# A fused linear-attention and ELU-MLP kernel: paced loads, fewer load buffers, and four output blocks of the first tile at once

## The chip, the core and the metric

The kernel runs on one core of a Trainium2 chip. TensorE (PE) multiplies, VectorE (DVE) and ScalarE (ACT) work on tiles elementwise, GpSimd (POOL) does a few elementwise products and issues the casting loads, SyncE (SP) issues the output stores and the transposes that the DMA crossbar makes. The metric is the device time of one execution in microseconds (us); lower is better.

## The reference

Two layers. The first is linear attention with decay, in 4 batches of 8 heads, 768 positions, head size 64. The second is an MLP with an ELU between its two products, 3072 tokens by 512, inner size 2048.

```python
for b in range(nb):                                  # blocks of 64 positions
    intra = einsum('bhic,bhjc->bhij', qb, kb) * Dmask
    intra = einsum('bhij,bhjd->bhid', intra, vb)
    inter = einsum('bhid,bhde->bhie', qb * lam_pow, kv_state)
    out[:, :, sl] = intra + inter
    kb_dec = kb * rev_pow
    kv_state = lam_block * kv_state + einsum('bhsd,bhse->bhde', kb_dec, vb)
x = out.transpose(0, 2, 1, 3).reshape(3072, 512)
h = x @ w_in
g = where(h > 0, h, exp(min(h, 0)) - 1)
return g @ w_out
```

## The kernel before

**Chunks and tiles.** The positions are cut into 24 chunks of 128 positions of one batch: chunk `g` is position block `g // 4` of batch `g % 4`. Seven tiles of 4, 2, 4, 4, 4, 4 and 2 chunks (`TS`) go through the MLP: tile 0 holds chunks 0 to 3, tile 1 chunks 4 and 5, tile 2 chunks 6 to 9, and so on.

**Attention of a chunk.** q, k and v come in natural layout by casting loads from POOL (`emit_load`, L72); `qn`, `kn`, `vn` are 12 buffers of two chunks each, so every chunk has its own. `att_T` transposes q and k on PE (L218) and `att_Te` copies the result to SBUF on ScalarE (L230); for the chunk pairs listed in `XT` (L615) `att_xT` lets the DMA crossbar transpose instead, from SP (L274). `att_S` (L305) makes scores `psS`, `att_mask` (L317) multiplies them by the decay mask into `P` on VectorE, `att_O` (L331, L339) adds `P`·v and q·state into `psO`, `att_X` (L358, L360) copies that to `xt`, the MLP's input. `att_kd` (L292) scales k, `att_U` (L377) makes the state's increment `psU`, `att_st` (L411, L413) adds it, `att_tmp` (L394) makes the decayed old state on POOL for the next chunk of that batch.

**MLP.** `mm1(t, n)` makes block n of 16 of h for tile t in PSUM (`psH`, L430; for tiles of two chunks two blocks in one bank, L445). ScalarE makes `e = exp` (L456) and `r = relu` (L460), VectorE joins them to `g = min(e - 1, r)` (L473); in three blocks of tile 0 VectorE does it from `e` and `psH` in two steps (L468, L471). `mm2(t, i, n)` adds g's block n times w_out's block n into `psM` of output block i (L505); at n = 15 the result is copied (L519, L521) and stored by SP (L522). e, r and the output copies have three buffers each.

**PSUM.** Three tags share the eight banks: S (four banks, two tiles of two), M and H (two banks each). psH of tile 0 alternates between M and H for n below 8; all other psH are in H, psM in M, and in stage B psM of a block above 1 would be in H.

**Order.** Nothing is scheduled by a planner: every engine runs its instructions in the order of this program. First comes a hand-written part for chunks 0 to 3, with `warm` matmuls on constant data between. Then `steps` (L644) lists, in order, a step name, the mm1 of that step and the mm2 of that step; `at` hangs attention work and loads on step names. Steps ('A', 0..15) are tile 0's mm1, ('B', ...) have no mm1, (1, n) to (6, n) belong to tiles 1 to 6, ('E', 0) is the end. Within a step: mm1 with e and r, then what hangs on the step, then g, then the mm2. `visit(g, s0, s1, s2)` hangs a pair's transposes and kd on s0, scores and masks on s1, products, state and copies on s2.

**Loads.** `LOADS` (L113) is the order of all loads on POOL, weights (`wi` in seven pieces, `wo` in four of four blocks) and two kd products among them. The first 17 are issued at once, ten more after the hand-written part, the last eight at steps of tiles 1 and 2 (L641). A load is only held back when POOL's queue for transfers is full.

The lines that a reader needs most:

```python
    NB = 12
    for s, a, b in [((1, 0), 27, 28), ((1, 4), 28, 29), ..., ((2, 9), 34, 35)]:
        at(s, run_loads, LOADS[a:b])
    for s, m1, m2 in steps:
        ...
            er = mm1(t, n, alt=t == 0 and n in (2, 4, 6))
        do(s)
        if er:
            elu(t, n, *er)
        for t2, i2, n2 in m2:
            mm2(t2, i2, n2, "H" if t2 == 0 and m1 is None and i2 > 1 else "M")
```

Of the kernel before, what the change touches and what calls it, by code (L numbers as in the profile page):

```python
# [7 lines left out]
FP32 = mybir.dt.float32  # L8
# [7 lines left out]
def kernel(  # L16
# [39 lines left out]
    NB = 12  # L56
# [56 lines left out]
    LOADS = [(0, 1, 'q'), (0, 1, 'k'), (0, 1, 'v'), (1, 1, 'q'), (1, 1, 'k'), (1, 1, 'v'), (2, 1, 'q'), (2, 1, 'k'), (3, 1, 'q'), (3, 1, 'k'), (2, 1, 'v'), (3, 1, 'v'), ('wi', 0), ('wi', 1), ('wi', 2), ('wi', 3), ('wi', 4), ('wi', 5), ('kd', 0), ('wi', 6), ('kd', 2), ('wo', 0), (4, 2), ('wo', 1), ('wo', 2), ('wo', 3), (6, 2), (8, 2), (10, 2), (12, 2), (14, 2), (16, 2), (18, 2), (20, 2), (22, 2)]  # L113
# [13 lines left out]
    run_loads(LOADS[:17])  # L127
# [54 lines left out]

    def late_up():
        nc.scalar.activation(ks[:], loglam[:], AF.Exp, scale=pos[:, 1:2])
        for hh in range(2):
            r = slice(hh * 64, (hh + 1) * 64)
            nc.scalar.copy(loglam_p[r, :], loglam[r, hh::2])
        nc.scalar.activation(up_p[:], loglam_p[:], AF.Exp, scale=float(L))
# [158 lines left out]
    def att_X(g, n, parts=1):  # L347
# [5 lines left out]
        for j in range(parts):  # L353
            c = slice(j * w, (j + 1) * w)
            dst = xt[t][:, c, i * L : (i + n) * L].rearrange("p h (n l) -> p n h l", n=n)
            if g < B:
                copy = nc.vector.tensor_copy if g == 0 else nc.scalar.copy
                copy(out=dst, in_=po[:, :, c])  # L358
                continue
# [41 lines left out]
    def att_st(g):  # L401
# [5 lines left out]
        for hh in range(2):  # L407
            r = slice(hh * 64, (hh + 1) * 64)
            if c == 0:
                copy = nc.scalar.copy if g in (2,) else nc.vector.tensor_copy  # L410
# [24 lines left out]
    def mm1(t, n, alt=False):  # L435

        MT = TS[t] * L
        if MT == 256:
            if n == 0:
                gt[t] = msb.tile([128, NF, MT], FP16, tag="g", bufs=2, name=f"g{t}")  # L440
            pH = ps.tile([128, 2 * MT], FP32, tag="H", bufs=2, name=f"psH{t}_{n}")
# [35 lines left out]
    def mm2_last(t, i):  # L477
# [4 lines left out]
        for x, (w, tag) in enumerate([(384, 'M'), (128, 'H')]):  # L482
# [7 lines left out]
            o = msb.tile([128, w], FP32, tag="osb", bufs=3, name=f"osl{x}")  # L490
# [6 lines left out]
    def mm2(t, i, n, tag="M"):  # L497
# [15 lines left out]
        o = msb.tile([128, DM], FP32, tag="osb", bufs=3, name=f"osb{t}_{i}")  # L513
# [3 lines left out]
        else:  # L517
# [4 lines left out]
            nc.sync.dma_start(out=out[t0 : t0 + L, :], in_=o[:])  # L522
        psM.pop((t, i))

    def warm(k, tag="M"):
# [4 lines left out]
        for _ in range(k):  # L530
            nc.tensor.matmul(
                pw[:], lhsT=ident16[:], rhs=any16, start=True, stop=True
            )

    warms = []
    any16 = ident16[:].unsqueeze(1).broadcast_to([128, 4, 128])
# [16 lines left out]
    W = [5, 2, 3, 0, 1, 1, 0, 0, 1, 1, 0]  # L553
# [7 lines left out]
    late_up()  # L561
    warm(W[2])
    att_S(0)
    att_mask(0, 2)
    warm(W[3])
    op_T(1, "q")
    op_Te(1, "q")
    warm(W[4])
    op_T(1, "k")
    op_Te(1, "k")  # L570
    att_O(0, 1, "M")
    att_X(0, 1)
    warm(W[5])
    att_S(1)
    att_mask(1, 2)
    op_T(2, "q")
    op_Te(2, "q")
    warm(W[6])
    op_T(2, "k")
    op_Te(2, "k")  # L580
    warm(W[7])
# [3 lines left out]
    att_mask(2, 2)  # L585
    att_O(1, 1, "M")
    att_X(1, 1)
    warm(W[8])
    att_T2(3, "k", "H")
    warm(W[9])  # L590
    att_S(3)
    att_mask(3, 2)
    att_O(2, 1, "M")
    att_X(2, 1)
    late_qs(0, 2)
    warm(W[10])
    for n in range(0):
        mm1_mm(0, n, 0, 3 * L, "MH"[n % 2])
    att_OX2(3, "H")
    for n in range(0, 1):  # L600
        mm1_mm(0, n, 0, 3 * L, "MH"[n % 2])
    late_qs(2, HP)
    for n in range(1):
        mm1_mm(0, n, 3 * L, 4 * L)

    run_loads(LOADS[17:27])
# [8 lines left out]
    XT = {10: (1, 12), 12: (2, 4), 14: (2, 12), 16: (3, 4), 18: (3, 12), 20: (4, 4), 22: (4, 12)}  # L615
# [23 lines left out]
    for g, vs in [(4, (('A', 12), ('A', 14), ('B', 1))), (6, ((1, 0), (1, 4), (1, 6))), (8, ((1, 8), (1, 12), (1, 14))), (10, ((2, 0), (2, 2), (2, 5))), (12, ((2, 8), (2, 10), (2, 13))), (14, ((3, 0), (3, 2), (3, 5))), (16, ((3, 8), (3, 10), (3, 13))), (18, ((4, 0), (4, 2), (4, 5))), (20, ((4, 8), (4, 10), (4, 13))), (22, ((5, 0), (5, 2), (5, 5)))]:  # L639
        visit(g, *vs)  # L640
    for s, a, b in [((1, 0), 27, 28), ((1, 4), 28, 29), ((1, 8), 29, 30), ((1, 12), 30, 31), ((2, 0), 31, 32), ((2, 3), 32, 33), ((2, 6), 33, 34), ((2, 9), 34, 35)]:  # L641
        at(s, run_loads, LOADS[a:b])

# [42 lines left out]
```

## Time and profile before

| what | value |
| --- | --- |
| median of 4 runs | 216.37 us (215.71 to 216.66) |
| the profiled execution | 216.66 us, of which the span from the first to the last instruction is 214.8 us |
| PE busy | 203.2 us, 95% of the span, 1650 matmuls |
| weight loads (PEld) | 105.8 us, 49% |
| VectorE busy | 151.3 us, 70% |
| ScalarE busy | 128.2 us, 60% |
| GpSimd busy | 77.6 us, 36% |
| software-made DMA queue (POOL's loads) | 80208 packets, 13.63 MB written, 85.1% of 16 engines' span |
| hardware-made DMA queue (SP and ScalarE) | 18384 packets, 9.90 MB, 21.3% |

How to read it: busy is the time in which an engine had an instruction running. A matmul is written down with its modelled end, 0.38 us for 512 columns, while the next can start 0.216 us after it, so a full PE row can still hide a slower pace. The chain of waits goes back from the last instruction, at each step to what released it. Step names like (1, 10) are those of `steps`.

### The profile page before, as it was taken

Reading aid. Unit: us, or ns where it says so; the run is one execution under the profiler, and the core shown is the slowest. Engines: PE = TensorE matmul, PEld = TensorE weight load, DVE = VectorE, ACT = ScalarE, POOL = GpSimd, SP = SyncE. Lnnn points to the kernel's source line nnn. Section 1 sums busy time; section 2 is a strip of 40 time slices with the busy share of each in tenths; the row PEclk is TensorE's granted clock in tenths of the full one; section 3 lists DMA queues with packets and bytes.
Section 4 is the critical chain, followed back from the end, with each engine's and each line's share of the span. In section 5 each row is a group of like instructions: output and inputs, shape, how many; then the busy total and the mean of one; then the engine's idle time right before and its main releaser. Section 6 shows DMA issues by size and latency. Waiting matters only on the chain.

```text
span 214.8 us, 4091 instructions
## 1 busy us (share of the span) xinstructions
PE 203.2 (95%) x1650; PEld 105.8 (49%) x1650; DVE 151.3 (70%) x193; ACT 128.2 (60%) x241; POOL 77.6 (36%) x76
## 2 busy tenths in 40 slices
PE   5878979999999999999999999999999999999994
PEld 1343435556764544545444545445445444555543
DVE  6766999976999999997986786765565533423221
ACT  6948798337566767666465566466456567454510
POOL 8999958469398956344400000000000000000000
PEclk9999999999999999999999999999999999999999
DMA  5999999999999999999993313314211011111112
GB/s 38 144 156 184 203 168 196 189 162 143 156 131 155 208 153 167 133 156 179 184 141 82 68 49 92 57 49 102 50 49 52 0 49 49 53 49 49 49 52 99
DMA packets 98756, 23.87 MB, mean 111 GB/s; under 512 B 90928, under 2 KB 95792, under 8 KB 98736
## 3 DMA queue, kind: packets, MB, share of 16 engines
q0 software_dynamic: 80208, 13.63, 85.1%
q1 hardware_dynamic: 18384, 9.90, 21.3%
q8 instruction: 13, 0.21, 0.4%
q10 hardware_dynamic: 144, 0.07, 0.1%
q14 instruction: 7, 0.06, 0.1%
HBM read 27.27 MB, written 6.29 MB: 156 GB/s over the span
## 4 chain that ended last, share of the span: by engine, by line
PE 58%; POOL 16%; DMA 14%; issue 5%; DVE 4%; ACT 0%; POOLq 0%; DVEq 0%
PE psM L505 29%; PE psH L430 15%; PE psH L445 7%; DMA qn<-in_q_dram 5%; DMA kT<-kn 5%; DMA wo<-in_moe_w_out_dram 4%; POOL qn L72 3%; POOL kn L72 3%; POOL vn L72 3%; POOL wi L97 2%; POOL tmp L394 2%; DVE g L473 2%; PE psO L331 2%; POOL kd L292 2%; PE psM L485 2%
## 5 line engine op out<-in xcount | busy, mean ns | idle before, releaser
L473 DVE SCALAR_TENSOR_TENSOR g<-e,r 128x512 f16<-128x512 f32 x93 | 69.1, 760 | 40.4 <-ACT r L460 40.1
L456 ACT ACTIVATE e<-psH 128x512 f32<-128x512 f32 x96 | 57.5, 599 | 63.2 <-PE psH L430 46.5
L505 PE MATMUL psM<-wo,g 128*128 128x512 f16 x368 | 93.8, 380 | 0.9 <-DMA wo<-in_moe_w_out_dram 0.8
L430 PE MATMUL psH<-xt,wi 128*128 128x512 f16 (+2 forms) x324 | 81.2, 376 | 1.0 <-DVE g L471 0.5
L460 ACT ACTIVATE r<-psH 128x512 f16<-128x512 f32 x93 | 55.3, 595 | 0.1
L505 PEld LDWEIGHTS <-g 128*128 128x128 f16 x368 | 34.3, 98 | 38.5 <-DMA wo<-in_moe_w_out_dram 1.3
L430 PEld LDWEIGHTS <-wi 128*128 128x128 f16 x324 | 31.2, 98 | 38.8 <-issue 1.2
L317 DVE TENSOR_TENSOR P<-psS,mask 128x1024 f16<-128x1024 f32 (+1 forms) x28 | 28.7, 1065 | 4.1 <-PE psS L305 3.9
L394 POOL TENSOR_TENSOR tmp<-st,up_p 64x512 f32<-64x512 f16 x16 | 20.1, 1259 | 14.2 <-DVE st L413 13.4
L72 POOL DMA_DIRECT2D vn<-in_v_dram x14 | 15.2, 1095 | 5.5 <-issue 4.4
L72 POOL DMA_DIRECT2D qn<-in_q_dram x14 | 15.6, 1116 | 4.1 <-issue 3.7
L72 POOL DMA_DIRECT2D kn<-in_k_dram x14 | 15.3, 1092 | 4.5 <-issue 3.1
L445 PE MATMUL psH<-xt,wi 128*128 128x256 f16 x128 | 16.6, 273 | 0.0
L360 DVE TENSOR_TENSOR xt<-psO,qs 128x1024 f16<-128x1024 f32 x10 | 12.2, 1220 | 4.9 <-PE psO L339 4.7
L445 PEld LDWEIGHTS <-wi 128*128 128x128 f16 x128 | 12.5, 98 | 4.9
L521 ACT COPY osb<-psM 128x512 f32<-128x512 f32 x12 | 7.1, 590 | 11.8 <-PE psM L505 11.8
L292 DVE TENSOR_TENSOR kd<-kn,ks 128x1024 f16<-128x1024 f16 x8 | 12.4, 1548 | 0.6 <-DMA kn<-in_k_dram 0.6
L331 PE MATMUL psO<-P,vn 128*64 128x128 f16 x184 | 11.9, 223 | 0.5 <-DVE P L317 0.5
L331 PEld LDWEIGHTS <-vn 128*64 128x64 f16 x184 | 9.6, 109 | 4.9 <-issue 4.1
L413 DVE TENSOR_TENSOR st<-tmp,psU 64x512 f16<-64x512 f32 x16 | 10.9, 680 | 0.2
L339 PE MATMUL psO<-qT,st 128*64 128x128 f16 x160 | 10.2, 219 | 0.0
L339 PEld LDWEIGHTS <-st 128*64 128x64 f16 x160 | 9.0, 110 | 0.0
(62 smaller groups left out, 105.6 us busy)
## 6 DMA issues: line engine op xcount, KB each, us to landing
out_dram<-osb SPq DMA_DIRECT2D x23, 256.0 KB, 2.3
qn<-in_q_dram POOLq DMA_DIRECT2D x10, 256.0 KB, 12.2
kn<-in_k_dram POOLq DMA_DIRECT2D x10, 256.0 KB, 14.2
vn<-in_v_dram POOLq DMA_DIRECT2D x10, 256.0 KB, 16.2
wo<-in_moe_w_out_dram POOLq DMA_DIRECT2D x4, 512.0 KB, 14.0
wi<-in_moe_w_in_dram POOLq DMA_DIRECT2D x2, 512.0 KB, 9.4
wi<-in_moe_w_in_dram POOLq DMA_DIRECT2D x3, 256.0 KB, 7.1
qn<-in_q_dram POOLq DMA_DIRECT2D x4, 128.0 KB, 4.6
```

The source lines that it names most:

```text
L72: nc.gpsimd.dma_start(out=dst, in_=src[b : b + n, :, rows].rearrange("b h p d -> p (b h) d"))
L292: e.tensor_tensor(out=kd[:].rearrange("p (n h) d -> p n h d", n=n), in0=heads(kn, g, n).rearrange("p (n h) d -> p n h d", n=n), in1=ks_b, ...
L317: nc.vector.tensor_tensor(out=P[:, :, c], in0=s[:, :, c], in1=(mask if g < B else mask1)[:, :, c], op=ALU.mult,)
L331: nc.tensor.matmul(po[r, i, hp, :], lhsT=v_of(g + i, 2 * hp + hh), rhs=P[:, hh, hp, :], start=True, stop=(c == 0), skip_group_check=True,)
L339: nc.tensor.matmul(po[r, i, hp, :], lhsT=st[(g + i) % B // 2][c % 2][:, (g + i) % 2, hp, r], rhs=qT[g + i][:, hp, :], start=False, stop=Tr ...
L394: e.tensor_tensor(out=tmp[r], in0=old[r, :, :, r], in1=up_p[r].unsqueeze(1).unsqueeze(3).broadcast_to([64, 2, HP, 64]), op=ALU.mult,)
L430: nc.tensor.matmul(pH[:, lo:hi], lhsT=wi[:, kk, j * 128 : (j + 1) * 128], rhs=xt[t][:, kk, lo:hi], start=(kk == 0), stop=(kk == HP - 1),)
L445: nc.tensor.matmul(pH[:, x * MT : (x + 1) * MT], lhsT=wi[:, kk, j * 128 : (j + 1) * 128], rhs=xt[t][:, kk, :], start=(kk == 0), stop=(kk = ...
L456: nc.scalar.activation(e[:], pH[:], AF.Exp)
L460: nc.scalar.activation(r[:], pH[:], AF.Relu)
L473: nc.vector.scalar_tensor_tensor(out=g, in0=e[:], scalar=-1.0, in1=r[:], op0=ALU.add, op1=ALU.min)
L505: nc.tensor.matmul(pm[:], lhsT=gt[t][:, n, i * L : (i + 1) * L], rhs=wo_t[wo_at[n][0]][:, wo_at[n][1], :], start=(n == 0), stop=(n == NF - 1),
```

## The change

- The buffers of q, k and v go from 12 to 8 pairs, so that chunks 16 to 23 take the places of chunks 0 to 7. The output copies have 6 buffers for 3.
- `LOADS`: in the first twelve all q and k come before all v. kd of chunks 0/1 now stands behind wi piece 3, kd of 2/3 behind piece 5; wo's second piece comes ahead of the loads of chunks 4/5.
- The loads of chunks 8/9 hang on ('B', 2); those of chunks 10 to 23 hang on later steps than before, each behind a one-element copy on POOL (`paced_load`) from the g that the step's predecessor makes.
- Chunks 8/9 are transposed by the crossbar, at ('B', 13).
- The hand-written part is reordered: all transposes and scores run ahead of the products with v; the warm matmuls have 2 columns instead of 512 and are 34 instead of 14; chunk 3's k is transposed in one piece; `ks`, `up_p` and `qs` are made at other places; the copies of chunks 0 to 2 into `xt` are all on ScalarE, and the first state copies all on VectorE.
- `steps`: stage A has mm2 from A12 on only. Stage B has 14 steps instead of 5 and does all four output blocks of tile 0, two in M and two in H; before, blocks 2 and 3 ran in tile 1's steps. Tile 1's mm2 begin within tile 1, tile 2's within tile 2, and so on; before, each tile's mm2 ran in the next tile's steps. The first psH of tile 1 takes an M bank.
- The visits of chunks 4/5 and 6/7 move from A12 and (1, 0) to ('B', 1) and ('B', 12).
- The stores of chunks 18 and 19 are issued by POOL instead of SP.

```diff
-    NB = 12
+    NB = 8
...
-    LOADS = [(0, 1, 'q'), (0, 1, 'k'), (0, 1, 'v'), (1, 1, 'q'), (1, 1, 'k'), (1, 1, 'v'), (2, 1, 'q'), (2, 1, 'k'), (3, 1, 'q'), (3, 1, 'k'), (2, 1, 'v'), (3, 1, 'v'), ('wi', 0), ('wi', 1), ('wi', 2), ('wi', 3), ('wi', 4), ('wi', 5), ('kd', 0), ('wi', 6), ('kd', 2), ('wo', 0), (4, 2), ('wo', 1), ('wo', 2), ('wo', 3), (6, 2), (8, 2), (10, 2), (12, 2), (14, 2), (16, 2), (18, 2), (20, 2), (22, 2)]
+    LOADS = [(0, 1, 'q'), (0, 1, 'k'), (1, 1, 'q'), (1, 1, 'k'), (2, 1, 'q'), (2, 1, 'k'), (3, 1, 'q'), (3, 1, 'k'), (0, 1, 'v'), (1, 1, 'v'), (2, 1, 'v'), (3, 1, 'v'), ('wi', 0), ('wi', 1), ('wi', 2), ('wi', 3), ('kd', 0), ('wi', 4), ('wi', 5), ('kd', 2), ('wi', 6), ('wo', 0), ('wo', 1), (4, 2), ('wo', 2), ('wo', 3), (6, 2), (8, 2), (10, 2), (12, 2), (14, 2), (16, 2), (18, 2), (20, 2), (22, 2)]
...
+    def late_ks():
+        nc.scalar.activation(ks[:], loglam[:], AF.Exp, scale=pos[:, 1:2])
...
-                copy = nc.vector.tensor_copy if g == 0 else nc.scalar.copy
+                copy = nc.vector.tensor_copy if g in () else nc.scalar.copy
...
-                copy = nc.scalar.copy if g in (2,) else nc.vector.tensor_copy
+                copy = nc.scalar.copy if g in () else nc.vector.tensor_copy
...
-            pH = ps.tile([128, 2 * MT], FP32, tag="H", bufs=2, name=f"psH{t}_{n}")
+            pH = ps.tile(
+                [128, 2 * MT], FP32, tag="M" if (t, n) in ((1, 0),) else "H", bufs=2,
+                name=f"psH{t}_{n}",
+            )
...
-        o = msb.tile([128, DM], FP32, tag="osb", bufs=3, name=f"osb{t}_{i}")
+        o = msb.tile([128, DM], FP32, tag="osb", bufs=6, name=f"osb{t}_{i}")
...
-            nc.sync.dma_start(out=out[t0 : t0 + L, :], in_=o[:])
+            (nc.gpsimd if T0[t] + i in (18, 19) else nc.sync).dma_start(
+                out=out[t0 : t0 + L, :], in_=o[:]
+            )
...
-                pw[:], lhsT=ident16[:], rhs=any16, start=True, stop=True
+                pw[:, 0:2], lhsT=ident16[:], rhs=any16[:, 0:2], start=True, stop=True
...
-    W = [5, 2, 3, 0, 1, 1, 0, 0, 1, 1, 0]
+    W = [10, 4, 3, 1, 2, 1, 2, 1, 3, 2, 2, 3]
...
+    late_qs(2, 3)
+    warm(W[10])
     att_O(2, 1, "M")
     att_X(2, 1)
-    late_qs(0, 2)
-    warm(W[10])
...
+    late_qs(3, 4)
+    warm(W[11])
     att_OX2(3, "H")
...
-    run_loads(LOADS[17:27])
+    run_loads(LOADS[16:27])
...
-    XT = {10: (1, 12), 12: (2, 4), ...
+    XT = {8: ('B', 13), 10: (1, 12), 12: (2, 4), ...
...
-    for g, vs in [(4, (('A', 12), ('A', 14), ('B', 1))), (6, ((1, 0), (1, 4), (1, 6))), (8, ((1, 8), (1, 12), (1, 14))), ...
+    for g, vs in [(4, (('B', 1), ('B', 4), ('B', 7))), (6, (('B', 12), (1, 0), (1, 4))), (8, ((1, 6), (1, 10), (1, 14))), ...
...
-    for s, a, b in [((1, 0), 27, 28), ((1, 4), 28, 29), ((1, 8), 29, 30), ((1, 12), 30, 31), ((2, 0), 31, 32), ((2, 3), 32, 33), ((2, 6), 33, 34), ((2, 9), 34, 35)]:
-        at(s, run_loads, LOADS[a:b])
+    def paced_load(s, items):
+        t, n = s
+        if t not in ("A", "B"):
+            w = 2 if TS[t] == 2 else 1
+            src = gt[t][0:1, n - w, 0:1] if n else gt[t - 1][0:1, NF - 1, 0:1]
+            nc.gpsimd.tensor_copy(pace[:], src)
+        run_loads(items)
+    for s, a, b in [(('B', 2), 27, 28), ((1, 2), 28, 29), ((1, 10), 29, 30), ((2, 3), 30, 31), ((2, 11), 31, 32), ((3, 3), 32, 33), ((3, 11), 33, 34), ((4, 3), 34, 35)]:
+        at(s, paced_load, s, LOADS[a:b])
```

The list `steps`, at the places that matter (a step is its name, its mm1, its mm2 as tile, output block, n):

```diff
-(('A', 10), (0, 10), [(0, 0, 0), (0, 1, 0)])
...
-(('B', 0), None, [(0, 0, 6), (0, 1, 6), (0, 0, 7), (0, 1, 7)])
...
-((1, 0), (1, 0), [(0, 2, 0), (0, 3, 0), (0, 2, 1), (0, 3, 1)])
...
-((2, 0), (2, 0), [(1, 0, 0), (1, 0, 1)])
...
+(('A', 12), (0, 12), [(0, 0, 0), (0, 1, 0)])
...
+(('B', 0), None, [(0, 2, 0), (0, 2, 1), (0, 2, 2), (0, 2, 3)])
+(('B', 1), None, [(0, 3, 0), (0, 3, 1), (0, 3, 2), (0, 3, 3)])
+(('B', 2), None, [(0, 0, 4), (0, 1, 4), (0, 2, 4), (0, 3, 4)])
...
+(('B', 13), None, [(0, 2, 14), (0, 3, 14), (0, 2, 15), (0, 3, 15)])
+((1, 0), (1, 0), [])
+((1, 2), (1, 2), [])
+((1, 4), (1, 4), [])
+((1, 6), (1, 6), [(1, 0, 0), (1, 1, 0), (1, 0, 1), (1, 1, 1)])
...
+((2, 8), (2, 8), [(2, 0, 5), (2, 1, 0)])
...
+((3, 3), (3, 3), [(2, 2, 1), (2, 2, 2), (2, 2, 3), (2, 2, 4), (2, 2, 5)])
```

## The prediction, made before the changed kernel was run

> **What bounds the kernel now.** I read the 40 slices of the page first, then the chain of waits, then the timeline at each place where the chain leaves TensorE.
>
> ```profile
> PE   5878979999999999999999999999999999999994
> DVE  6766999976999999997986786765565533423221
> POOL 8999958469398956344400000000000000000000
> DMA  5999999999999999999993313314211011111112
> ```
>
> A slice is 5.4 us. From slice 8 (43 us) to the end PE is full; before that it has holes, while VectorE (slices 5 to 8), GpSimd and the DMA engines are full. The DMA engines stay full to slice 20 (108 us), long after PE has stopped waiting for them.
>
> ```profile
> 21.08 9.16 DMA wo<-in_moe_w_out_dram
> 30.28 0.60 PE psM L505 x2
> ...
> 57.05 0.89 PE psT L218 x16
> ...
> 101.33 10.26 DMA kT<-kn
> 111.64 0.62 PE psS L305 x16
> ```
>
> Columns: start, length, what. The chain goes through loads until 30 us and then almost wholly through matmuls. One later place is a transfer: a crossbar transpose of 10.26 us that the scores of a pair wait for.
>
> Consecutive 128x512 matmuls start 0.216 us apart (four in 0.86). Against that pace the timeline's start times show these losses after the first psH matmul at 17.53: 0.31 at 21.31 (wi), 0.66 at 24.07, 0.47 at 28.47, 0.95 at 30.28 (wo), 0.64 at 34.02 (kn), 0.23 at 37.85, 0.63 at 41.63 (P), 0.21 at 47.44 (kn), 0.26 at 66.15 (xt), 0.54 at 111.64 (kT). The sum is 4.9 us, 3.9 of it before 42 us. New order alone can win little more than that, plus what the first 17.5 us give.
>
> **Head.** Twelve loads are issued in both orders, 0.87 us each, and the twelfth lands at 15.85 (landings are the semaphore updates in the trace). It was chunk 3's v and still is. Then come its product (0.3) and the copy in halves (ScalarE 0.36, VectorE 0.42), so the first psH matmul moves from 17.53 to 16.9; scores and masks no longer stand between. The moved kd products stay behind wi 3 and wi 5 on POOL, some 0.8 us earlier than at 16.55 and 19.23. The 34 small warm matmuls cost between 0.025 and 0.13 each (the weight load's row); the longest run after the last key is three, so 0 to 0.4 us. I take 0: they run while v loads, which land 0.87 us apart. The copies of tile 0 now all on ScalarE (0.58 for 0.69) lie in the same cover; without it they cost 0.1. The same cover takes the moved small ScalarE steps (ks 0.3, loglam_p and up_p 0.6, four qs of 0.4); the last qs can hold the half copy by at most its 0.4.
>
> ```profile
> 1.65 2.31 PE L531 MATMUL psW<-ident 128*128 128x512 f16 x5 [1.65 <-DVE ident L139]
> 17.53 3.64 PE L430 MATMUL psH<-xt,wi 128*128 128x384 f16 x20
> 19.23 1.92 POOL L292 TENSOR_TENSOR kd<-kn,ks 128x1024 f16<-128x1024 f16 x1
> 19.73 2.58 DVE L473 SCALAR_TENSOR_TENSOR g<-e,r 128x512 f16<-128x512 f32 x2 [1.67 <-ACT r L460]
> 24.07 1.89 PE L430 MATMUL psH<-xt,wi 128*128 128x512 f16 x8 [0.49 <-DVE g L471]
> 33.91 6.30 POOL L394 TENSOR_TENSOR tmp<-st,up_p 64x512 f32<-64x512 f16 x4
> ```
>
> The five warm matmuls start 0.43 us apart: half pace. From 8.5 us on the pace is full. **A rule that speaks against this edit** is in the Trainium skill, "TensorE: Matmul & The Clock Gate", Part 1: the clock is half until about 3.4 us of sustained matmul activity has passed. Whether two columns count as activity no row shows. If they don't, the clock opens at the end of the first wholly busy window after 16.9; windows of 3.4 us counted on from 8.4 give 22.1. The real transposes, scores and products fill 2 to 2.3 us of each window at half pace, the small ones up to 0.9 more by their weight loads, against about 2.8 us in the window that opened the clock before. By the row stage A starts at full pace; by the rule it ends 1.2 us later. I take the row and keep the rule as a rival.
>
> **Stage A (16 psH blocks of tile 0).** No mm2 is now due before A12, and chunk 4's transposes, scores and masks leave this stage; the second st copy comes to VectorE. PE's own work, 16 x 0.86 + 8 x 0.216 + 0.72 for two psU, is 16.2 us, but the ELU sets the pace. VectorE begins when kd of the second pair lets it go: the timeline has g at 19.73 with 2.58 for two where two take 1.37, beside a POOL kd of 1.92. With kd 0.8 earlier I set the begin to 20.4. To g of block 10 it does 8 x 0.68 + 3 x 1.77 (the m and max pairs) + 4 x 0.69 (st) = 13.5, hence 33.9. e has three buffers, so e of block 13 waits for that g and starts at about 34.2; its r ends at 35.3; block 15 takes that PSUM bank and ends at 36.5; two mm2 more: **36.9**. The tmp products on POOL (33.91, 6.30) stretch the last g from 0.68 to about 1.5, which PE doesn't wait for. Wi pieces land at 25.1 and 27.7 as before and bind less. Before, by 36.9, PE had done 16.1 us of the same work; stage A by itself wins nothing.
>
> **Stage B.** 56 mm2 (12.1), the transposes of chunks 4/5 (0.9), their scores (0.55), products with state (1.27), and the transposes of 6/7 (0.9): 15.7 us, so tile 1 starts at 52.6. The bytes ahead of wo's last piece are the same, so it lands near 44.0, as now; what PE does by then is different, since all four blocks can use pieces 0 to 2 (48 mm2 instead of 24). Block 8 of g is reached at 43.5, wo 2 lands near 41; piece 3 is reached at 48. No wait is left. Before, the same work is done at 45.91 + 32 x 0.216 + 0.9 + 0.21 = 53.9. **Gain 1.3**, which is the losses at 37.85, 41.63 and 47.44 plus 0.2. The psM of blocks 2 and 3 take H banks: the first psH of tile 1 goes to M (freed two steps earlier), the next waits for a copy of 0.6 behind 1.4 us of PE work.
>
> **Chunks 8/9 by crossbar**: 16 transposes leave PE, **0.89** by the chain's row at 57.05, and two copies of 1.02 leave ScalarE. What can be late is kT. Loads of 8/9 are issued when POOL leaves the tmp products (40.2), and land behind v of 6/7 (49.0) 1.8 us apart: q 50.8, k 52.6. The pair of transposes took 9.8 to 12.9 us in the full DMA (58.44 to 68.25, 80.34 to 93.24), 4.6 in the quiet one (116.16 to 120.74). Here the DMA is free from 54.4 until chunk 10: I take 8, so 59.3. Its scores are due at 61.5. No wait; at 12.9 it would be 2.7. On SP the transposes stand ahead of two output stores of tile 0, which wait with them; six output buffers cover that.
>
> **Paced loads.** The one-element copy on POOL is not in the trace: 0.1 (memset row) to 1.26 (tmp row); I take 0.1, eight in 200 us. It waits for a g; behind it on POOL stand three issues (3.5 us) and a tmp product, for which crossbar transposes on SP and an st sum on VectorE wait. Chunk 14 is issued near 73, its transpose is due at 88; an idle queue needs about 7 us, so nobody waits. The skill's "DMA: Bandwidth & Descriptors", Rules for kernel authors, says the contrary of pacing: issue early, wait late. Early issue has a row against it here: kT of 10.26 us and a loss of 0.54 at 111.64. By the rule with today's latency (k 14.2 us) k of 14 lands at 89 and its scores, due at 98, still stand. By the row, with 5.5 us of transfers in every 10 to 15, the wait at 111.64 goes: **gain 0.54**. Eight buffers: chunk 16 takes chunk 0's, done 40 us before. Six output buffers and two stores from POOL (1.1 us each, nothing behind them): 0.
>
> **Tile 1, the cost.** PE now does tile 1 up to tile 2 in 15.3 us instead of 20.5. VectorE does not shrink: from 53.9 two P (2.35), two g, X (1.2), st (1.4), g, kd (1.3 to 2.06), two g, two P, two g, X: to 68.8. PE is there at 67.9, so **0.9** for the 0.26 of now. After that the work per step is as before, and mm2 uses g three steps old: the g ended at most 4.1 us after its r in tile 2, three steps with a visit last over 4.
>
> **Sum**: 1.3 + 0.89 + 0.54 - (0.9 - 0.26) = 2.1. The profiled execution took 216.66 (span 214.8), so 214.6 there; the median of the runs is 0.29 lower, so **214.3** in its terms. All times below are too.
>
> **Rivals.**
> (a) *A lighter ELU chain*: if kd on POOL doesn't hold the first g, stage A ends at 35.9, or nearer to PE's own limit: 1 to 2 us more, 213.3 to 212.3. For it: kd's place is new. Against: POOL is full to 28 us. 0.22.
> (b) *Cold clock*, as above: 1.2 less gain, 215.5. 0.12.
> (c) *kT of chunks 8/9 late*: 12.9 instead of 8 us; 2.7 of waiting, in which VectorE makes good its 0.64: 214.3 + 2.1 = 216.4, no change. For it: three of the four pairs in the full DMA took over 11. 0.12.
> (d) *VectorE becomes the bound, slower*. Place: from (1, 0) to tile 3. If its work there runs at contended length (kd 2.06, two g at 1.48 beside tmp), X of chunk 8 comes 2.4 later, a wait of 3.3; in tile 2 VectorE's 16 x 0.69 + 2 x 6.5 + 1.4 = 25.4 stands against PE's 24.5, and with lags of three steps instead of a tile 0.9 of it reaches PE. Then 1.3 + 0.89 + 0.54 - 3.04 - 0.9 = -1.2: 217.6. It decides once VectorE is over 2 us behind at (1, 14). For it: VectorE is at 9 in slices 11 to 18. Against: pacing takes POOL's descriptor work out of that stretch. 0.13.
>
> The forecast has 0.41. **How the numbers follow**: within 0.3% of the median (0.65 us, about what can be told from no change) is 215.72 to 217.02. Faster: the forecast, nearly all of it (0.39), (a) 0.22, more than half of (b), little of (c): 0.74. Same: the rest of (b), most of (c) and of the forecast's edge: 0.13. Slower: (d), 0.13. The range is 212.3, the end of (a), to 216.7, just over (c); outside lie (d) and a little beyond (a).
>
> **What would show it**: first psH at 16.9 at 0.216 pace (0.43 would be b); last psH of tile 0 near 36.5; no wait at wo's last piece; tile 1 at 52.6 (51 would be a); wait before psS of chunk 8 (c); a loss of about 0.9 before tile 2's first psH (3 would be d); none near 111. It is wrong altogether if wo's last piece lands after 48, since then stage B waits in one block.

## The result, and the profile after

The changed kernel takes 215.96 us (median of 43 runs, 215.63 to 216.84); the kernel before, over 64 runs beside it, 216.33. The ratio is 0.9982, with a 95% interval of 0.9973 to 0.9992: a gain of 0.4 us (0.2 to 0.6) where 2.1 were forecast. The time lies inside the range given, but among the changes under 0.3%, which had a chance of 0.13. Its profiled execution took 216.06 us with a span of 214.3, against 216.66 and 214.8. A few executions show a lower recorded clock and are slower; the ratios leave them out and can differ by some 0.1% from the quotient of the medians given.

The slices of the page of the changed kernel, then its chain of waits (share of the span by engine):

```profile
PE   5888989999997999989999999999999999999994
DVE  6764997854999999999698688676557634353321
POOL 8999956951496447091650510600000000011000
DMA  6999999999999969999399792499601111011112
...
PE 61%; DVE 17%; POOL 10%; DMA 6%; issue 3%; ACT 0%; DVEq 0%; POOLq 0%
```

VectorE now has a hole in slices 8 and 9 (43 to 54 us) and is full from 10 to 18; PE has a dent in slice 12 that it did not have. The DMA row has gaps from slice 14 on (14, 19, 24) and goes on to slice 28 instead of 20: that is the pacing. And VectorE holds 17% of the chain that ends last, where before it held 4%. In time order that chain holds nothing but VectorE's work and short issue times from 53.5 to 96.5 us. Its beginning and end (start, length, what):

```profile
53.54 1.10 issue
54.65 1.22 DVE P L319
55.86 1.01 DVE g L478 x2
56.98 1.22 DVE xt L362
...
94.14 2.37 DVE g L478 x2
98.02 1.02 PE psM L510 x4
```

The busy times of the engines by stretch, of the kernel before and then of the changed one (stretch, us; then busy us and count of PE, PEld, DVE, ACT and POOL; clock, DMA share, GB/s; the DMA share adds up the times of packets, so it can pass 1):

```profile
46.00:54.00 8.00, 7.96 (x82) 5.53 (x82) 5.30 (x6) 5.61 (x10) 7.60 (x7) 1.00 1.54 154
54.00:62.00 8.00, 8.00 (x117) 5.97 (x114) 7.73 (x10) 5.50 (x10) 5.04 (x5) 1.00 2.33 138
62.00:70.00 8.00, 7.90 (x91) 4.30 (x92) 7.78 (x9) 4.56 (x10) 7.41 (x7) 1.00 2.04 157
86.00:98.00 12.00, 12.00 (x112) 6.01 (x110) 11.73 (x16) 7.21 (x15) 5.44 (x6) 1.00 2.00 151
```

```profile
46.00:54.00 8.00, 8.00 (x69) 4.71 (x68) 4.61 (x7) 3.83 (x6) 2.07 (x2) 1.00 2.31 192
54.00:62.00 8.00, 8.00 (x113) 5.99 (x111) 7.94 (x10) 5.20 (x11) 5.47 (x5) 1.00 1.22 173
62.00:70.00 8.00, 6.63 (x80) 4.20 (x79) 7.94 (x9) 2.55 (x5) 5.67 (x7) 1.00 1.80 155
86.00:98.00 12.00, 11.20 (x96) 5.25 (x93) 11.94 (x15) 7.16 (x14) 6.62 (x6) 1.00 1.35 123
```

VectorE was nearly full in both kernels; what differs is whether TensorE has to wait for it. Before, it doesn't (12.00 of 12.00 in the last line); after, it does. The waits stand in TensorE's timeline of the changed kernel (in brackets: idle before, counted from the modelled end of the matmul ahead, and what ended it):

```profile
65.78 0.25 PE L333 MATMUL psO<-P,vn 128*64 128x128 f16 x2 [0.39 <-DVE P L319]
66.91 0.25 PE L333 MATMUL psO<-P,vn 128*64 128x128 f16 x2 [0.49 <-DVE P L319]
69.25 1.04 PE L432 MATMUL psH<-xt,wi 128*128 128x512 f16 x4 [0.48 <-DVE xt L362]
96.55 0.60 PE L510 MATMUL psM<-wo,g 128*128 128x512 f16 x2 [0.80 <-DVE g L478]
```

In the kernel before, tile 2 starts without such a bracket:

```profile
66.15 1.04 PE L430 MATMUL psH<-xt,wi 128*128 128x512 f16 x4
```

**The balance.** Count as a loss every start of a matmul that comes over 0.1 us later than the pace of the one before it allows, from the first psH on:

| | before | after |
|---|---|---|
| first psH | 17.53 | 17.00 |
| losses to 40 us | 3.26 | 2.64 |
| losses 40 to 56 | 0.83 | 0 |
| losses 56 to 72 | 0.26 | 1.86 |
| losses 72 to 100 | 0 | 1.11 |
| losses 100 to 140 | 0.54 | 0 |
| sum | 4.89 | 5.61 |
| first psH of tile 1 / 2 / 3 | 45.91 / 66.15 / 90.94 | 52.10 / 69.25 / 94.29 |
| last matmul | 211.60 | 211.11 |

PE starts 0.53 earlier and has 0.90 less to do, loses 0.72 more, and smaller gaps take 0.22: 0.49 at the last matmul. (Tile 1 itself starts later because tile 0's projections now all stand before it.)

The first row is not firm. In fifteen profiled executions with this head, of the changed kernel and of those below, the first psH falls between 16.82 and 17.55 us, and the last psH block of tile 0 starts at 34.50 to 34.67 in all of them. So the 0.53 lies within what the same head shows from one execution to the next, and the end of stage A does not follow it. Tile 1 starts between 51.70 and 52.63 in the nine of them with nothing changed ahead of it. From there on two executions of the changed kernel agree within 0.02 us (159.01 and 159.03 to the last matmul), so the experiments are read by their distance from tile 1's start where that matters.

**A mistake in what stands above.** The warm matmuls of the changed kernel do not have 2 columns. The index 0:2 falls on the middle axis of a 128 x 4 x 128 tile, which is 256 columns, as its timeline shows:

```profile
1.65 2.32 PE L538 MATMUL psW<-ident 128*128 128x256 f16 x10 [1.65 <-DVE ident L139]
```

### The profile page after: what moved, and what is told of

The parts are those of the page before. It is cut to its first block, busy times and chain, and to the rows that moved or that the text cites. A ratio compares the mean times of both kernels' runs of the same rounds, so it can differ in the third digit from the quotient of the medians.

```text
span 214.3 us, 4112 instructions
## 1 busy us (share of the span) xinstructions
PE 203.0 (95%) x1650; PEld 106.3 (50%) x1650; DVE 151.1 (71%) x193; ACT 125.9 (59%) x238; POOL 82.6 (39%) x85
## 4 chain that ended last, share of the span: by engine, by line
PE 61%; DVE 17%; POOL 10%; DMA 6%; issue 3%; ACT 0%; DVEq 0%; POOLq 0%
PE psM L510 31%; PE psH L432 19%; DVE g L478 8%; DMA kn<-in_k_dram 6%; DVE P L319 4%; PE psH L450 4%; DVE st L415 2%; POOL wi L97 2%; POOL qn L72 2%; POOL kd L294 2%; DVE xt L362 2%; PE psS L307 2%; POOL kn L72 2%; PE psM L490 2%; POOL vn L72 2%
## 5 line engine op out<-in xcount | busy, mean ns | idle before, releaser
L478 DVE SCALAR_TENSOR_TENSOR g<-e,r 128x512 f16<-128x512 f32 x93 | 71.4, 784 | 37.6 <-ACT r L465 37.2
L432 PE MATMUL psH<-xt,wi 128*128 128x512 f16 x320 | 81.2, 379 | 2.1 <-ACT r L465 0.8
L432 PEld LDWEIGHTS <-wi 128*128 128x128 f16 x320 | 30.8, 98 | 40.7 <-issue 2.1
L396 POOL TENSOR_TENSOR tmp<-st,up_p 64x512 f32<-64x512 f16 x16 | 21.0, 1312 | 5.6 <-DVE st L415 4.9
L527 POOL DMA_DIRECT2D out_dram<-osb x2 | 1.1, 572 | 55.9 <-ACT osb L526 51.9
L654 POOL COPY pace<-g 1x1 f16<-1x1 f16 x7 | 2.8, 398 | 45.0 <-DVE g L478 45.0
L72 POOL DMA_DIRECT2D kn<-in_k_dram x14 | 15.3, 1093 | 1.9 <-DMA wo<-in_moe_w_out_dram 1.9
L72 POOL DMA_DIRECT2D vn<-in_v_dram x14 | 15.3, 1110 | 1.7 <-DVE g L478 1.7
L450 PEld LDWEIGHTS <-wi 128*128 128x128 f16 x128 | 12.4, 98 | 4.2
L294 DVE TENSOR_TENSOR kd<-kn,ks 128x1024 f16<-128x1024 f16 x8 | 11.4, 1426 | 0.0
```

What stands on the lines that cost most here:

```text
L72: nc.gpsimd.dma_start(out=dst, in_=src[b : b + n, :, rows].rearrange("b h p d -> p (b h) d"))
L294: e.tensor_tensor(out=kd[:].rearrange("p (n h) d -> p n h d", n=n), in0=heads(kn, g, n).rearrange("p (n h) d -> p n h d", n=n), in1=ks_b, ...
L396: e.tensor_tensor(out=tmp[r], in0=old[r, :, :, r], in1=up_p[r].unsqueeze(1).unsqueeze(3).broadcast_to([64, 2, HP, 64]), op=ALU.mult,)
L432: nc.tensor.matmul(pH[:, lo:hi], lhsT=wi[:, kk, j * 128 : (j + 1) * 128], rhs=xt[t][:, kk, lo:hi], start=(kk == 0), stop=(kk == HP - 1),)
L450: nc.tensor.matmul(pH[:, x * MT : (x + 1) * MT], lhsT=wi[:, kk, j * 128 : (j + 1) * 128], rhs=xt[t][:, kk, :], start=(kk == 0), stop=(kk = ...
L478: nc.vector.scalar_tensor_tensor(out=g, in0=e[:], scalar=-1.0, in1=r[:], op0=ALU.add, op1=ALU.min)
```

## The experiments

Each kernel ran on one chip with the kernel before beside it; ratios are over that kernel, with 95% intervals. "Loss" is counted as in the table. Diffs are against the changed kernel unless said otherwise. A first control, the changed kernel again, gave 0.9978 (0.9965 to 0.9991) and its four waits at the same places with the same sizes, although its first psH came at 17.55 instead of 17.00:

> The changed kernel unaltered, as the control on the chip of the three runs that follow: time over that of before 0.9982, within its interval of 0.9973 to 0.9992 (about 216.0 us where before is 216.4); first scores of tile 3 at 94.3 us of the span; TensorE waits of 0.5 to 1.0 us at 65.8, 66.9, 69.3 and 96.6.

**1. Take work off VectorE, in blocks.**

```diff
-            if i % 2:
+            if i % 2 and t not in (1, 2):
...
-            at(s0, att_kd, g, 2, "p" if g in () else "a" if g in () else "v")
+            at(s0, att_kd, g, 2, "p" if g in () else "a" if g in (8, 10, 12) else "v")
```

> The changed kernel with work taken from VectorE between the start of tile 1 and the start of tile 3, and nothing else moved: the output copies of tiles 1 and 2 all on ScalarE (three of 0.69 us) and kd of the pairs 8/9, 10/11, 12/13 on ScalarE (1.2 to 2.1 us each), so about 6.5 us less on VectorE in a stretch where it is busy 7.9 of every 8 us. Theory 'VectorE is the bound from 54 to 97 us': TensorE's losses at 65.8, 66.9, 69.3 and 96.6 (2.8 us together) go nearly all, the time falls by 2 to 2.8 us, to 213.2 to 214.0, and VectorE shows idle time again between 62 and 98. Rival 'the losses come from the short distance between g and its mm2, or from late loads': the losses stay, the time moves by less than 0.5 us.

Measured: 1.0008 (0.9990 to 1.0026), no gain; the median is 0.5 us over that of the changed kernel (216.45 for 215.96). Tile 2 did start 16.28 us after tile 1 instead of 17.15 (losses at 56 to 72 down from 1.86 to 0.90), but losses at 72 to 100 rose from 1.11 to 2.40. ScalarE's and TensorE's timelines of this kernel say why:

```profile
70.03 2.43 ACT L292 ACTIVATE kd<-kn,ks 128x128 f16<-128x128 f16 x8
...
83.35 2.43 ACT L292 ACTIVATE kd<-kn,ks 128x128 f16<-128x128 f16 x8
```

```profile
73.47 1.02 PE L432 MATMUL psH<-xt,wi 128*128 128x512 f16 x4 [0.55 <-ACT r L465]
...
86.79 1.02 PE L432 MATMUL psH<-xt,wi 128*128 128x512 f16 x4 [0.77 <-ACT r L465]
```

Eight head-sized operations in one block hold r back by 2.4 us, and with it the PSUM bank that TensorE's next psH needs. So this run doesn't decide on the theory; a relief without the block was needed.

**2. A like relief, spread.** The output copies as in 1; per pair of chunks 8 to 13, four heads in one VectorE operation of half the size, the other four on ScalarE, one at each of four steps.

```diff
-            if i % 2:
+            if i % 2 and t not in (1, 2):
...
+            if g in KD:
+                at(s0, kd_half, g)
+                for x, s in enumerate(KD[g]):
+                    at(s, kd_head, g, H // 2 + x)
```

> VectorE relieved in tiles 1 and 2 without a long block on ScalarE: the output copies of these tiles all on ScalarE, and of the scaled keys of chunks 8 to 13 the first four heads on VectorE (one operation of half the size) and the last four on ScalarE, one head in each of four steps. Theory (VectorE is what bounds tiles 1 and 2 of the changed kernel): some 2 x 6 half-sized output copies of 0.7 us and half of three 1.6-us scalings leave VectorE there, the waits of 0.56, 0.66 and 0.64 us at 65 to 69 shrink to below 0.2, tile 3's first scores come at 91.8 to 92.8 instead of 94.3, and the time falls by 1.5 to 2.5 us against the changed kernel, to 213.5 to 214.5. Rival (the bound is the chain from scores to P to output, not the load, or ScalarE has no room): tile 3's first scores within 0.5 us of 94.3, the time within 0.6 of the changed kernel's.

Measured: 0.9921 (0.9894 to 0.9948), 1.3 us under the changed kernel on the same chip (214.80 for 216.10). Tile 3 starts 41.61 us after tile 1 instead of 42.19; losses at 56 to 72 are 1.23, at 72 to 100 0.66. Less than expected: VectorE is still at 7.91 of 8 us in 62 to 70, so it binds less but binds.

**3. Only the order of eight projections.**

```diff
-((3, 0), (3, 0), [(2, 0, 13), (2, 1, 8), (2, 0, 14), (2, 1, 9)]), ((3, 1), (3, 1), [(2, 0, 15), (2, 1, 10), (2, 1, 11), (2, 1, 12)])
+((3, 0), (3, 0), [(2, 1, 8), (2, 1, 9), (2, 1, 10), (2, 1, 11)]), ((3, 1), (3, 1), [(2, 0, 13), (2, 0, 14), (2, 0, 15), (2, 1, 12)])
```

> Only the order of eight projections of tile 2 at steps (3,0) and (3,1) is changed: the four of column half 1 that need nothing new come first, the three of chunk 13 to 15 later, so that TensorE has filler while VectorE is late with the normalised output at 94 to 97 us. Theory (VectorE is only about a microsecond late there and catches up): the wait of 0.96 and 0.14 us at 96.6 to 98 goes, the time falls by 0.9 to 1.1 us against the changed kernel, to about 215. Rival (the lateness is passed on to the next VectorE result): the wait moves by a step or two and the time stays within 0.3 us of the changed kernel's.

Measured: 0.9957 (0.9941 to 0.9973), 0.5 us under the changed kernel on the same chip (215.56 for 216.10). The wait didn't go; counted from tile 1's start it came 1.4 us later and was smaller, 0.67 at 98.5 for 1.11 at 96.6 to 98. In this execution tile 1 started 0.53 later than in the changed kernel, and the losses at 56 to 72 were the same 1.87. Between theory and rival: filler covers what VectorE is late by, up to the amount of filler.

**4. Both.**

> The relief of VectorE in tiles 1 and 2 and the new order of eight projections together. Theory: with the relief tile 3 starts without a wait and the order adds nothing or little: 213.3 to 214.3 us, tile 3's first scores at 91.8 to 92.8. Rival (relief buys nothing): the time of the new order alone, about 215.

Measured: 0.9913 (0.9889 to 0.9937), 214.65 us, a little over the 213.3 to 214.3 expected; losses at 72 to 100 down to 0.23, tile 3 at 93.68, tile 4 at 125.61 for 127.11. Beside the relief alone (214.80) the intervals overlap: that the order adds to it is not shown.

**5. The relief in the kernel before.** The edit of 2, against the kernel before (the single heads of chunks 8 and 9 at the steps of its own visit).

> The kernel before, with the same relief of VectorE in its tiles 1 and 2 (output copies of tiles 1 and 2 on ScalarE, half of the key scaling of chunks 8 to 13 on ScalarE, one head at a step). Theory (it is the change that makes VectorE bind there): TensorE loses only 0.26 between 56 and 100 us in the kernel before, so at most that is won, time over that of before 0.998 to 1.002. Rival (VectorE's load costs the same in both kernels): a gain of 1.2 us as in the changed kernel, 0.994.

Measured: 1.0019 (1.0005 to 1.0033): nothing won, a little lost. The losses at 56 to 72 are 1.29 for 0.26, of which 0.79 is a wait for kT of chunk 10 and 0.29 one for kd, so the relief brought waits of its own here. But there was only 0.26 to win: in the kernel before TensorE hardly waits for VectorE, which is nearly as full. The two orders differ in two ways there. TensorE had 20.0 us of work between the starts of tiles 1 and 2, beside which VectorE's chain has to run; now it has 15.3. And each tile's projections ran in the next tile's steps, so a g that came late delayed nobody up to 100 us.

**6. The crossbar's share, without and with the relief.** Chunks 8 and 9 are transposed by TensorE again.

```diff
-    XT = {8: ('B', 13), 10: (1, 12), ...
+    XT = {10: (1, 12), ...
```

> The changed kernel with chunks 8/9 transposed on TensorE at step (1, 6) again instead of by the DMA crossbar: 0.89 us more on TensorE and 2.0 us more on ScalarE, nothing on VectorE. Theory 'VectorE is the bound there': TensorE only fills time in which it waits, so the time rises by 0 to 0.3 us. Rival 'TensorE's work decides there, as the prediction counted it': it rises by 0.9 us.

> Relief and new order as in the kernel that held both, but chunks 8 and 9 transposed on TensorE again (0.89 us of TensorE, 1.02 of ScalarE). In the changed kernel this put tiles 2 to 6 no later. Theory (VectorE hid the worth of the crossbar): with VectorE relieved a part of the 0.89 shows, tile 3 starts 0.3 to 0.9 later than the 93.68 of both, time 0.3 to 0.9 longer. Rival (VectorE still binds, or TensorE's waits still absorb it): tile 3 within 0.2 of 93.68.

Measured, without relief: 1.0030 (1.0014 to 1.0046), some 0.7 us over the changed kernel by the medians (216.67 for 215.96, on different chips), which is near the rival's 0.9. But the traces put none of it where the transposes are. TensorE has 0.89 more work and 0.99 less loss at 56 to 100, and from tile 1's start to the last matmul both kernels take 159.0 us. In tiles 1 and 2, then, the saved transposes only made TensorE wait instead. The extra time lies after the last matmul: the span ends 3.83 us after it, 3.15 in the changed kernel. The output's last landing follows as quickly as before (2.23 and 2.24), but SyncE's closing drain begins 2.89 us after the last matmul instead of 2.32. No run here shows why.

With the relief: 0.9967 (0.9954 to 0.9980), against 0.9913; counted from tile 1's start, tile 3 and the last matmul come 0.53 later, and the same 0.7 follows behind (3.84). So 0.5 of the 0.89 becomes real once VectorE is relieved.

**7. No pacing.** The one-element copies are taken out, so that each load goes as soon as GpSimd reaches it.

```diff
-            nc.gpsimd.tensor_copy(pace[:], src)
+            pass
```

> The changed kernel without the one-element copies on GpSimd that hold the loads of chunks 10 to 23 back (their places in the program stay): GpSimd issues as soon as it comes to them and a buffer of the eight pairs is free. Prediction's count: the DMA engines are full again and a crossbar transpose is late as at 111 us before, 0.3 to 0.6 us slower. Theory 'VectorE is the bound until 97 us and TensorE afterwards': the same or slightly faster (0 to 0.4 us), since the descriptor work comes earlier, when VectorE is idle or waits anyway, and tmp products come free at once; the loss at 96.6 shrinks if the g beside tmp get shorter.

Measured: 1.0234 (1.0200 to 1.0269), and both expectations fell. TensorE's timeline of this kernel:

```profile
64.79 1.03 PE L307 MATMUL psS<-qT,kT 64*128 64x128 f16 x16 [3.61 <-DMA kT<-kn]
65.76 1.89 PE L510 MATMUL psM<-wo,g 128*128 128x512 f16 x4
67.44 1.43 PE L450 MATMUL psH<-xt,wi 128*128 128x256 f16 x8
```

The load of chunks 10 and 11 goes out at 48.9 instead of 57.1 us, and kT of 8 and 9 now lands 11.1 us after its issue (53.60 to 64.74); paced, it took 4.5 (52.89 to 57.39). The scores of chunk 8 come 3.8 us late and take 1.03 us, where 16 of them take 0.62 in the changed kernel; the next four projections start 0.40 to 0.43 us apart instead of 0.216. The stretches of the same kernel give the clock with it (columns as above):

```profile
65.70:67.50 1.80, 1.80 (x9) 0.65 (x6) 1.80 (x2) 0.00 (x0) 0.00 (x0) 0.50 1.33 132
```

From 64.81 to 68.20 us the same view gives 0.50 throughout, 1.00 behind it. Two more losses follow, 1.58 at 90.6 and 0.52 at 101.3. Pacing is worth some 5 us here (1.0234 against 0.9982), not the 0.54 that I gave it.

**8. Warm matmuls of really two columns.**

```diff
-                pw[:, 0:2], lhsT=ident16[:], rhs=any16[:, 0:2], start=True, stop=True
+                pw[:, 0, 0:2], lhsT=ident16[:], rhs=any16[:, 0, 0:2], start=True, stop=True
```

> The changed kernel with warm matmuls of really 2 columns (the change's warm matmuls turned out to have 256). Theory 'columns that stream open the clock': the head runs at half pace up to one full window after the first psH matmul, near 22 us; the start of tile 1 moves by about 1.2 us, and as VectorE is the bound afterwards and idles in stage B, 0.5 to 1.2 us of it reach the end. Theory 'weight loads count as activity': full pace from about 8.5 us or a window later, no change (under 0.2 us).

Measured: 1.0081 (1.0052 to 1.0109), tile 1 2.3 us later (54.42) and the last matmul 2.3 later. None of it is absorbed on the way, against my expectation: tile 2 starts 17.16 us after tile 1, as in the changed kernel (17.15), with losses of 1.87 there. The timeline shows psH beginning at half pace:

```profile
16.34 0.24 PE L538 MATMUL psW<-ident 128*128 128x2 f16 x3
16.50 0.64 PE L264 MATMUL psO<-P,vn 128*64 128x128 f16 x8
17.64 5.53 PE L432 MATMUL psH<-xt,wi 128*128 128x512 f16 x18 [0.49 <-ACT xt L269]
```

18 matmuls in 5.53 us: 0.43 apart until 20.6, then 0.216. The clock column of this stretch reads 1.00 only because the trace has no clock record before 20.67, so here the half pace is seen in start times. This is my rival (b), and it agrees with the rule that I had against the edit, in the Trainium skill, "TensorE: Matmul & The Clock Gate", Part 1: there about 3.4 us of sustained matmul activity open the clock, here full pace came 3.0 us after the long matmuls began. It would have cost nearly twice what I wrote; the changed kernel escaped it because its warm matmuls are 128 times as wide as I read them.

**9. Does VectorE's idle time in stage B matter?** First try: two psH blocks of tile 1 are moved into it (blocks 0 and 1 of tile 0 are finished two steps earlier for it, tile 1's other psH move up, its first three take M banks, and the two paced loads of tile 1 wait for the g that now comes at their step). Of the list:

```diff
-(('B', 11), None, [(0, 0, 14), (0, 1, 14), (0, 0, 15), (0, 1, 15)])
-(('B', 12), None, [(0, 2, 12), (0, 3, 12), (0, 2, 13), (0, 3, 13)])
+(('B', 11), (1, 0), [(0, 2, 10), (0, 3, 10), (0, 2, 11), (0, 3, 11)])
+(('B', 12), (1, 2), [(0, 2, 12), (0, 3, 12), (0, 2, 13), (0, 3, 13)])
```

> The changed kernel with two psH blocks of tile 1 moved up into stage B: tile 0's output blocks 0 and 1 are finished first (B8, B9), their PSUM banks go to tile 1's first three psH, of which two run in B11 and B12 beside the last projections of blocks 2 and 3. No work is added or taken away. Theory (VectorE's lateness in tiles 1 and 2 comes from the idle 3.4 us that it has at 46 to 54 us, in which all four blocks run and no psH): two ELU results of 0.68 us are done in that gap, VectorE is 1.3 us less late, the losses at 65 to 69 fall from 1.86 to 0.6 or so, the time by 0.8 to 1.3 us against the changed kernel. Rival (the chain of scores, P and output sets tile 2's start and not VectorE's load): P and xt are as late as before, TensorE runs out of other work earlier, the time is the same or up to 0.5 longer.

> The early psH blocks, the relief of VectorE in tiles 1 and 2 and the new order of eight projections together. If they add up: 1.45 us from relief and order as measured, and 0.6 to 1.0 of what is left of the losses at 56 to 72 (1.23): 213.6 to 214.1 us. If the early psH only move the wait: 214.6.

Measured: 1.0021 (0.9987 to 1.0056), and with relief and order 1.0013 (0.9976 to 1.0051). The rival was right here: the blocks push the scores of chunk 6 back by 2 us and its P with them (55.47 for 53.51), losses at 56 to 72 stay (1.78), and the later load of chunks 10 and 11 adds a wait for kT (1.03 at 73.9, 2.44 at 74.3 in the second, after which the granted clock is 0.50 until 77.5). Inconclusive for the idle gap itself.

Second try: the visit of chunks 6 and 7 earlier, nothing else.

```diff
-(6, (('B', 12), (1, 0), (1, 4)))
+(6, (('B', 10), ('B', 12), (1, 2)))
```

> The changed kernel with only chunks 6 and 7 visited earlier: their transposes at B10 instead of B12, their scores at B12 instead of (1,0), their products, output and state at (1,2) instead of (1,4). No work is added or taken away, no psH moves. Theory (VectorE is late in tiles 1 and 2 because it sits idle at 47 to 53 us until the scores of 6 and 7 come): the two P start near 51 instead of 53.5, the losses at 65 to 69 fall from 1.86 to 0.6 or less, the time by 1.0 to 1.8 us against the changed kernel (214.2 to 215.0). Rival (what was idle stays idle: loads or PSUM banks hold the visit, or the earlier visit only makes TensorE wait for k of 6 and 7, landed at 47.4): no gain, within 0.4 us of the changed kernel.

> The same earlier visit in the kernel with relief of VectorE and new order. Theory: the losses at 66 to 69 (1.23) fall below 0.5 and the time to 213.3 to 214.1, the fastest of all. Rival: 214.6, as without it.

Measured: 1.0316 (1.0268 to 1.0363) and 1.0299 (1.0259 to 1.0340), 7.0 and 6.4 us over the kernel before, yet the first half of the theory holds: P starts at 51.04, the losses at 56 to 72 fall from 1.86 to 0.30, and tile 2 starts at 67.90, earlier than in any other kernel with the new list of steps, although tile 1 starts 0.8 later. Then 6.6 us are lost at once:

```profile
78.00 1.04 PE L307 MATMUL psS<-qT,kT 64*128 64x128 f16 x16 [6.47 <-DMA kT<-kn]
```

GpSimd's timeline of the same kernel shows the cause:

```profile
57.75 2.48 POOL L396 TENSOR_TENSOR tmp<-st,up_p 64x512 f32<-64x512 f16 x2 [8.05 <-DVE st L415]
60.29 0.53 POOL L654 COPY pace<-g 1x1 f16<-1x1 f16 x1
60.77 1.21 POOL L72 DMA_DIRECT2D qn<-in_q_dram  x1
...
64.24 0.18 POOL L654 COPY pace<-g 1x1 f16<-1x1 f16 x1
64.36 1.15 POOL L72 DMA_DIRECT2D qn<-in_q_dram  x1
```

The tmp products now stand ahead of the load of chunks 10 and 11 in GpSimd's order, so it leaves at 60.8 instead of 57.1. The next load's pace copy finds its g already made and lets it go at once, at 64.4: two loads run together while the crossbar works on 10 and 11. The pacing is undone by a delay of 3.7 us.

Third try: that one load is put ahead of the visit.

```diff
+    at((1, 2), paced_load, (1, 2), LOADS[28:29])
     for g, vs in [(4, ...
```

> The early visit of chunks 6 and 7 as before, and the paced load of chunks 10 and 11 at (1,2) put ahead of that visit on GpSimd, so that it no longer stands behind the tmp products and comes near 55.7 us, not 60.9. Theory (the wait of 6.6 us for kT of chunk 10 came from that load sitting 0.6 us before the next one; the filled gap of VectorE is a gain): kT of 10 and 11 in time, the losses at 56 to 72 at about 0.3 as in the first early visit, the time 1.0 to 1.8 us under the changed kernel: 214.2 to 215.0. Rival (the crossbar transposes of 10 and 11 are late whatever the load's place, since SP issues them behind others): again 3 us or more of waiting near 75.

> The same in the kernel with relief of VectorE and new order of eight projections. Theory: 213.3 to 214.1, the fastest of all. Rival: a late kT again, over 216; or no gain over the relief and the order alone, 214.6.

Measured: 0.9968 (0.9954 to 0.9982) and, with relief and order, 0.9905 (0.9877 to 0.9933), 214.26 us. No late kT, but both miss what the theory expected (214.2 to 215.0, 213.3 to 214.1). Of the 1.86 some 0.74 goes (loss 1.12), and tile 1 starts 0.9 later, 0.46 of it a wait before the scores of chunk 6. The rest of the 1.86 stays because the tmp products now run at 59.8 to 62.9, beside kd and two g, which VectorE pays for in its timeline:

```profile
59.94 2.05 DVE L294 TENSOR_TENSOR kd<-kn,ks 128x1024 f16<-128x1024 f16 x1
61.91 2.13 DVE L478 SCALAR_TENSOR_TENSOR g<-e,r 128x512 f16<-128x512 f32 x2
...
66.34 1.28 DVE L478 SCALAR_TENSOR_TENSOR g<-e,r 128x512 f16<-128x512 f32 x2
```

The last kernel of the list has the lowest ratio of all; against the one without the early visit (0.9913) the intervals overlap. The relief is shown to pay, and the order where it stands alone; the early visit beside them is not.

## Why the prediction was right and wrong

**Head: right, for a reason that was partly wrong.** First psH at 17.00 at full pace, 16.9 predicted; that the number fits so well is luck, since the same head gives 16.82 to 17.55. The clock held because the warm matmuls have 256 columns; with two the loss is 2.3, not 1.2 (experiment 8).

**Stages A and B: right in kind, a little small.** The last psH block of tile 0 starts at 34.5 and so ends near 35.4, 36.5 being predicted; nothing waits at wo's last piece, which landed at 43.56 (44.0 predicted); one wait of 0.37 for k of chunks 4/5, at 37.5, was not foreseen. Tile 1 starts at 52.10 for the predicted 52.6, so the term of 1.3 was 1.8 (52.63 at the latest in other executions, which would make it 1.3).

**Crossbar for 8/9: the transfer right, its worth wrong.** kT landed 4.5 us after its issue, at 57.39 (8 us and 59.3 taken), and nobody waited: rival (c) did not come about. But the 0.89 counted only as TensorE time; in the changed kernel it went into waiting for VectorE, by the traces of experiment 6.

**Pacing: sign right, size wrong.** The 0.54 at 111 us is gone, as said, and 0.52 comes back at 101 without pacing. What pacing holds back elsewhere, 3.8 us at 64.8 and 1.58 at 90.6, I counted as nothing, because I compared with the old order, in which 8 and 9 do not use the crossbar. The rule that I set against it (the Trainium skill, "DMA: Bandwidth & Descriptors", Rules for kernel authors: issue a DMA early and wait for it late) does not hold for this kernel, where early issue costs about 5 us (experiment 7). The copies are seven, not eight, at 0.40 us each.

**The step that failed** is the last term, "0.9 for the 0.26 of now. After that the work per step is as before". It was sized 0.64 net and measured 2.71 net: losses of 1.86 at 65 to 69 us and 1.11 at 96 to 98, less 0.26.

- At tile 2's start TensorE's side was right: 15.3 us of work from tile 1's start, measured 17.15 less 1.86 of waits. (For the old order I wrote 20.5; its trace has 20.0, which changes no term.) VectorE's side was short. Its chain begins with P, once TensorE has made the scores of chunk 6 behind tile 1's start, and ends with the xt of chunk 8. I had 14.9 us for it (53.9 to 68.8); it took 15.7 (53.51 to 69.20), and it began 1.4 after tile 1's start for my 1.3. The lengthened piece is two g of 2.97 us, for which my sum had 1.36; they run beside GpSimd's tmp products. (kd, for which I had allowed up to 2.06, took 1.21.) VectorE's and GpSimd's timelines of the changed kernel:

```profile
61.50 2.97 DVE L478 SCALAR_TENSOR_TENSOR g<-e,r 128x512 f16<-128x512 f32 x2
60.53 3.39 POOL L396 TENSOR_TENSOR tmp<-st,up_p 64x512 f32<-64x512 f16 x2
```

  Because this chain hangs on tile 1's start, what is won or lost ahead of tile 1 was kept: tile 1 came 0.5 later in experiment 3 and 2.3 later in experiment 8, and the losses at 56 to 72 were 1.87 both times. What TensorE saves inside the stretch is not, as the crossbar's 0.89 shows.
- "After that" was wrong by 1.11. My own line on the lag stood beside it: a g up to 4.1 us after its r against three steps of over 4 us. It left no margin. The three g at 94.14, again beside GpSimd's tmp, used it up at 1.27 us each; in the kernel before three g took 1.90 with no tmp beside them (third line):

```profile
94.14 3.81 DVE L478 SCALAR_TENSOR_TENSOR g<-e,r 128x512 f16<-128x512 f32 x3
94.70 2.69 POOL L396 TENSOR_TENSOR tmp<-st,up_p 64x512 f32<-64x512 f16 x2
90.67 1.90 DVE L473 SCALAR_TENSOR_TENSOR g<-e,r 128x512 f16<-128x512 f32 x3
```

With the measured sizes the sum is 1.8 + 0.89 + 0.54 - 2.71 = 0.5, and the span fell by 0.5. It is the mechanism of rival (d), VectorE as the bound, at some 70% of its price: 1.86 at the first place where (d) had 3.3, 1.11 at the second where it had 0.9. Of the lengths that (d) rests on, the two g came as written (1.48 each), kd did not.

Experiments 2 and 5 carry the cause: the relief wins 1.3 us in the changed kernel and nothing in the one before. That the g are long because of the tmp products is read from their times in the traces; no run moves the products away with all else kept. What stays open too is how much more an ideal order would give: in the best run 0.6 of the waits at 56 to 72 is left, and most of what remains is before 40 us.

## What to carry to other kernels

When a change shortens one engine's work in a stretch, look for the engine that was nearly full beside it, and ask from where its chain starts and at what lag its results are used. Time saved ahead of the chain's start is kept; time saved beside the chain turns into waiting. Here the order also moved the consumers of g closer, from a tile to three steps, and lateness that had been harmless became a wait. Relief pays in that chain, in small pieces; in one block it moved the wait to the engine that took it over. And a load that is held back by a result of the computation is part of the order: anything put ahead of it on its queue can bring two loads together again.

## What the runs showed of the hardware

- The crossbar suffered more from loads beside it than the loads did: the eight transposes of k took 4.0 us from issue to landing with paced loads and 9.5 without (medians), a load of k 8.3 and 11.3 (medians of the pages).
- A wait of 3.8 us was enough for the clock to fall: granted 0.50 and half pace from 64.8 to 68.2 us (experiment 7). After the wait of 6.6 us in experiment 9 half pace lasted from 78.0 to 83.8. The shortest wait that was followed by it is one of 2.4 us (experiment 9, first try with relief and order: granted 0.50 from 74.1 to 77.5); after one of 1.58 in experiment 7 the clock stayed at 1.00.
- A one-element copy on GpSimd took 0.40 us on average and 0.18 at the least; I had taken 0.1.
- Two g of 128x512 on VectorE took 1.28 us with only load issues on GpSimd beside them and 2.97 beside its tmp products (66.78 and 61.50 in the changed kernel).
- Two-column matmuls with their weight loads, in a mixed stream of transposes, scores and products, did not bring TensorE to full pace in 16 us; 256-column ones did.
